# A one-column matmul that reads k early, behind the first four score matmuls of a chunked retention + mish feed-forward kernel

## Chip, cores and metric

One NeuronCore of one Trainium2 chip runs the whole program. The metric is the device time of one execution in microseconds (us); lower is better. Before the change the median of 3 runs was 192.03 us (191.44 to 192.17).

## What is computed

The inputs q, k and v have 4 batches, 8 heads, 768 positions and 64 dimensions. Per batch and head a decaying state is carried along the sequence, and its read-out goes through a feed-forward layer with the mish activation:

```python
gamma = 1.0 - 2.0 ** (-5.0 - np.arange(H))
for t in range(S):
    state = gamma * state + outer(k[:, :, t], v[:, :, t])
    y[:, :, t] = scale * (q[:, :, t] @ state)
x = y.transpose(0, 2, 1, 3).reshape(B * S, H * D)      # 3072 x 512
h = x @ w_in                                           # 512 -> 2048
g = h * tanh(log1p(exp(h)))
out = g @ w_out                                        # 2048 -> 512
```

## The kernel before, in words

**Tiles.** The recurrence is cut into 24 chunks of 128 positions (six per batch). Within a chunk the sum over earlier positions becomes a masked score matrix, and what came before the chunk arrives through the state. From the third block on, a chunk is cut once more into two halves of 64 positions, and TensorE (PE) is used as four 64x64 quarters: the score, state and read-out matmuls there are all 64x64, written so that four neighbours use the four quarters.

**Blocks.** The work is done in 11 blocks: block 0 has the four chunks 0 to 3, every later block n has the two chunks 2n+2 and 2n+3 (256 tokens). A block's first feed-forward product (`g1_seven`, matmuls at L818) and second one (`seven`, matmuls at L954) are written as seven smaller products each, with sums of operands made by VectorE (DVE). The order of work is written out by hand: `steps_of` and `steps_of_first` (L1314, L1355) list what is done at each named step ("at1", "m1", "m3" and so on) between the products of a block, and instructions run on each engine in the order of the program. So the attention of block n+1 is done inside block n: its scores at step "m1" (`scores_two`, L500 to L511), its mask at "m5", its read-out at "m7" (`y_of`, L521).

**Outer products.** `y_of(n)` reads the state (L542) and applies the masked scores (L553). Then `outers` (L485 to L498) makes the products of k and v that move the state on, for the chunks that `outers_at(n)` names: the two chunks of block n+1. In blocks 2 and earlier it names one chunk only, and the second one's outer products are made at step "m1" by `scores_and_outer` (L587), ahead of the scores there. The stationary operand of each outer product is k in half precision (tile `qk`), so its weight load (LDWEIGHTS) needs k of that chunk.

**How k arrives.** `bring_k` (L418 to L427) copies k of a chunk from HBM and turns it to half precision on the way: two DMAs of 64 KB on GpSimd's (POOL's) queue, the first for heads 0, 2, 4, 6 and the second for heads 1, 3, 5, 7. From block 2 on, step "m3" asks for both chunks of the block three further on, four DMAs in a row. Chunk 10 is asked for at "m3" of block 1, and chunk 11 at the end of step "at1" of block 2, behind the casts there. `cast_q` and `cast_v` (L414, L431) write q and v in half precision on POOL, and `turn_by_dma` (L443) transposes q and k of a chunk with a DMA on SyncE's (SP's) queue into the tile `qkt`, from which the score matmuls read.

**Waits.** Where PE's first outer product has to wait both for its own engine and for a k DMA, a separate EVENT_SEMAPHORE instruction stands in PE's queue ahead of the weight load and takes one of the two.

Of the kernel before, what the change touches and what calls it, by code (L numbers as in the profile page):

```python
# [16 lines left out]
def kernel(  # L17
# [9 lines left out]
    nc = tc.nc  # L27
# [6 lines left out]
    HP = H // 2  # L34
# [23 lines left out]
    def toks(c):  # L58
        return slice(c * HB, (c + 1) * HB)
# [75 lines left out]
    loaded, cast, qkts, ats, ams, states, us, ys, sus = {}, {}, {}, {}, {}, {}, {}, {}, {}  # L135
# [364 lines left out]
    def scores_two(blk):  # L500
        a = first[blk]
        at = ats[a] = atps.tile([P, 2, 2, HP, HB], FP32, name="at", tag="at")
        for n in range(2):
            qt, kt = qkts[a + n]
            for j in range(HP):
                for c in range(2):
                    for x in range(2):
                        o = slice(64 * x, 64 * x + 64)
                        nc.tensor.matmul(  # L509
                            at[toks(c), x, n, j], kt[o, j, toks(c)], qt[o, j, toks(c)],  # L510
                            start=True, stop=True, skip_group_check=True)  # L511

    def mask_two(blk):
# [69 lines left out]
    def outers_at(blk):  # L583
        a = first[blk]
        return [a + 2] if blk <= TURN else [g for g in (a + 2, a + 3) if g < NCK]

    def scores_and_outer(g):  # L587
        outers([g], atps, "at")
        scores_two((g - CPB) // 2 + 1)
# [724 lines left out]
    def steps_of(blk):  # L1314
# [3 lines left out]
        else:  # L1318
# [8 lines left out]
            "at5": [(store_due, 3), (sums_a, blk, A)],  # L1327
            "g7": [(sums_a, blk, B)],
            "m1": only((scores_two, nb)),
            "m5": [*only((mask_two, nb)), (sums_b, blk)],  # L1330
            "m6": [(sums_c, blk), *then((gate_s, blk)), (cast_q, a + 1)],
# [80 lines left out]
```

## Time and profile before

| what | value |
|---|---|
| median of 3 runs | 192.03 us (191.44 to 192.17) |
| the profiled execution: its own time | 191.71 us |
| the profiled execution: its span | 189.8 us |
| PE matmuls busy | 183.3 us, 97% of the span |
| DVE busy | 156.7 us, 83% |
| ACT busy | 126.0 us, 66% |
| POOL busy | 94.7 us, 50% |

The span runs from the first to the last recorded instruction; the execution's own time has 1.9 us more around it. In the profile "PE" is a matmul and "PEld" the weight load ahead of it, "<-" reads "written from", and a line number is that of the kernel before. "DMA to landing" is the time from a DMA's issue to the last of its semaphore increments.

### The profile page before, as it was taken

The page shows a single profiled execution, that of the slowest core. Times are in us where ns is not written, and L with a number is a line of the kernel's source. Part 1 is how long each engine was busy: PE and PEld are TensorE (multiplying, and loading weights), DVE is VectorE, ACT ScalarE, POOL GpSimd, SP SyncE. Part 2 cuts the span into 40 slices and gives each one's busy share as a digit, 9 for nine tenths or more (in the row PEclk, how much of TensorE's full clock was granted, in tenths as well). Part 3 has the DMA queues.
Part 4 walks back from the last instruction along what each step waited for, and adds up shares of the span by engine and source line. Part 5 has one row for each costly group of instructions (what it writes and reads, how often), then busy time and mean ns, then how long its engine had stood idle before and what let it go on. Part 6 is the DMA issues. An engine that isn't in the chain of part 4 may idle for free.

```text
span 189.8 us, 7746 instructions
## 1 busy us (share of the span) xinstructions
PE 183.3 (97%) x3298; PEld 156.9 (83%) x3298; DVE 156.7 (83%) x330; ACT 126.0 (66%) x244; POOL 94.7 (50%) x135
## 2 busy tenths in 40 slices
PE   6989999999999999999999999999999999999992
PEld 2667546875988988988988988988988988989981
DVE  3997899889899698797897897797897897796662
ACT  3362699463893983894883883983884974975960
POOL 6570205696767937934934935915925923000000
PEclk9999999999999999999999999999999999999999
DMA  4999999999999999999996996996997953300203
GB/s 165 351 369 406 405 406 279 269 217 147 186 195 281 193 264 217 175 192 170 176 184 148 159 176 196 207 233 40 196 205 106 155 152 60 114 3 12 102 0 111
DMA packets 95521, 36.17 MB, mean 191 GB/s; under 512 B 82560, under 2 KB 88960, under 8 KB 95488
## 3 DMA queue, kind: packets, MB, share of 16 engines
q1 hardware_dynamic: 74112, 32.78, 73.7%
q0 software_dynamic: 21088, 2.62, 21.7%
q8 instruction: 25, 0.41, 0.9%
q10 hardware_dynamic: 288, 0.30, 0.4%
q14 instruction: 8, 0.07, 0.1%
HBM read 27.30 MB, written 6.29 MB: 177 GB/s over the span
## 4 chain that ended last, share of the span: by engine, by line
PE 94%; DVE 3%; issue 1%; POOL 0%; ACT 0%; POOLq 0%; DVEq 0%
PE h_ps L818 34%; PE o_ps L954 32%; PE h_ps L687 6%; PE o_ps L1207 5%; PE at L457 2%; PE h_ps L1055 2%; PE o_ps L1267 2%; PE y_ps L542 2%; PE at L509 2%; PE u_ps L495 2%; DVE am L329 2%; PE y_ps L553 2%; PE t_ps L264 1%; DVE osb L975 1%; PE at L322 0%
## 5 line engine op out<-in xcount | busy, mean ns | idle before, releaser
L838 DVE TENSOR_TENSOR hsum<-h_ps,hsnap 128x512 f32<-128x512 f32 x60 | 38.6, 685 | 9.7 <-ACT hsnap L828 6.8
L828 ACT COPY hsnap<-h_ps 128x512 f32<-128x512 f32 x60 | 32.1, 589 | 10.0 <-PE h_ps L818 9.7
L818 PEld LDWEIGHTS <-wsum 128*128 128x128 f16 x640 | 36.2, 98 | 0.2
L833 ACT ACTIVATE g<-hsum 128x512 f16<-128x512 f32 x60 | 34.6, 642 | 0.6 <-DVE hsum L838 0.2
L954 PEld LDWEIGHTS <-gsum 128*128 128x128 f16 x320 | 30.4, 98 | 3.7
L818 PE MATMUL h_ps<-xsum,wsum 128*128 128x128 f16 x480 | 30.2, 219 | 0.0
L954 PE MATMUL o_ps<-tmat,gsum 128*128 128x256 f16 x240 | 29.5, 273 | 0.0
L818 PEld LDWEIGHTS <-win 128*128 128x128 f16 x480 | 28.2, 98 | 0.9
L426 POOL DMA_DIRECT2D qk<-in_k_dram x36 | 27.6, 781 | 0.0
L954 PEld LDWEIGHTS <-g 128*128 128x128 f16 x248 | 22.7, 98 | 2.5
L414 POOL TENSOR_TENSOR qk<-qf,qvs 128x512 f16<-128x512 f32 x20 | 21.5, 1077 | 0.2 <-issue 0.2
L431 POOL TENSOR_TENSOR v<-vf,qvs 128x512 f16<-128x512 f32 x20 | 21.2, 1085 | 0.0
L954 PE MATMUL o_ps<-wout,g 128*128 128x256 f16 (+1 forms) x168 | 20.8, 267 | 0.0
L818 PE MATMUL h_ps<-xt,win 128*128 128x128 f16 x320 | 19.6, 219 | 0.0
L603 POOL TENSOR_TENSOR stc<-suc,gcv 128x256 f16<-128x256 f32 x15 | 9.9, 663 | 15.7 <-DVE suc L598 15.7
L560 ACT COPY hsum<-y_ps 128x512 f32<-128x512 f32 x9 | 5.3, 585 | 18.4 <-PE y_ps L553 18.4
L975 DVE TENSOR_TENSOR osb<-o_ps,snap 128x256 f32<-128x256 f32 (+1 forms) x32 | 13.0, 413 | 5.0 <-PE o_ps L954 2.5
L439 POOL COPY gate<-gsum 128x1 f16<-128x1 f16 x10 | 1.8, 185 | 26.8 <-DVE gsum L925 26.8
L963 ACT COPY snap<-o_ps 128x256 f32<-128x256 f32 x31 | 11.4, 371 | 5.5 <-PE o_ps L954 5.3
L818 PE MATMUL h_ps<-xsum,win 128*128 128x128 f16 x160 | 12.3, 220 | 0.0
L818 PE MATMUL h_ps<-xt,wsum 128*128 128x128 f16 x160 | 12.2, 219 | 0.0
L833 ACT ACTIVATE g<-h_ps 128x512 f16<-128x512 f32 x20 | 12.0, 598 | 0.0
(142 smaller groups left out, 310.6 us busy)
## 6 DMA issues: line engine op xcount, KB each, us to landing
vf<-in_v_dram SPq DMA_DIRECT2D x24, 256.0 KB, 6.0
out_dram<-osb SPq DMA_DIRECT2D x22, 256.0 KB, 3.5
qf<-in_q_dram SPq DMA_DIRECT2D x20, 256.0 KB, 4.9
wi<-in_moe_w_in_dram SPq DMA_DIRECT2D x3, 1024.0 KB, 10.5
wt<-in_moe_w_out_dram SPq DMA_DIRECT2D x3, 1024.0 KB, 9.3
qk<-in_k_dram POOLq DMA_DIRECT2D x36, 64.0 KB, 4.7
qfirst<-in_q_dram SPq DMA_DIRECT2D x2, 512.0 KB, 4.3
kf<-in_k_dram SPq DMA_DIRECT2D x4, 256.0 KB, 5.0
```

Of the source, the lines that this page charges most:

```text
L414: nc.gpsimd.tensor_tensor(by_head(g, room16(g)[0]), by_head(0, loaded[g][0]), f.broadcast_to((P, 2, HP, D)), op=ALU.mult)
L426: nc.gpsimd.dma_start(room16(g)[1][:, x::2], src[:, HP * x:HP * x + HP])
L431: nc.gpsimd.tensor_tensor(room16(g)[2], loaded[g][2], vs.unsqueeze(2).broadcast_to((P, H, D)), op=ALU.mult)
L603: by.tensor_tensor(stcs[g], sus.pop(g), decay, op=ALU.mult)
L687: nc.tensor.matmul(h_ps[:, j], win(s, f, bp), xt(blk, bp), start=(bp == 0), stop=(bp == NBP - 1))
L818: nc.tensor.matmul(h_ps[g][:, f], w(g, f, d), x(d), start=first and f == 0 and d == 0, stop=d == n - 1, skip_group_check=True)
L828: nc.scalar.copy(x, h_ps)
L833: nc.scalar.activation(gt[:, fb:fb + FPS, j * P:(j + 1) * P], h, AF.Mish, scale=inv_boost3)
L838: nc.vector.tensor_tensor(h, h_ps, x, op=ALU.add)
L954: nc.tensor.matmul(t, x(f), w(f)[:, c], start=first and f == 0, stop=f == n - 1, skip_group_check=True)
L963: nc.scalar.copy(x[:, c], t)
L975: nc.vector.tensor_tensor(dst[:, c], t, plus[:, c], op=ALU.add)
```

## The change

Inside `scores_two(blk)`, after the four matmuls of chunk n = 0 and head pair j = 0, one matmul is put in for each chunk that `outers_at(blk)` names. Its stationary operand is the first head's k of that chunk, 64 positions by 64 dimensions; its moving operand is one column of the transposed q. It writes one column of the score tile, at a place (chunk n = 1, last head pair) that a later score matmul of the same call overwrites, so no result depends on its value.

```diff
@@ scores_two
                             at[toks(c), x, n, j], kt[o, j, toks(c)], qt[o, j, toks(c)],
                             start=True, stop=True, skip_group_check=True)
+                if n == j == 0:
+
+                    for g in outers_at(blk):
+                        nc.tensor.matmul(
+                            at[:64, 0, 1, HP - 1, :1], cast[g][1][:64, 0], qt[:64, 0, :1],
                             start=True, stop=True, skip_group_check=True)
```

In the compiled program the other engines' instructions are the same and in the same order. On PE 15 pairs of weight load and matmul are added: one in the scores of block 2, and two each in the scores of blocks 3 to 9. Each added weight load waits for the first k DMA of its chunk. In return the first outer product of a chunk in `y_of` no longer waits for that DMA: in 8 places the two waits become one, and the separate EVENT_SEMAPHORE goes. The waits for each chunk's second k DMA stay where they were, in `y_of`.

More of the change, by code (lines that the diff above doesn't have):

```diff
@@ L510, in scores_two @@
                             at[toks(c), x, n, j], kt[o, j, toks(c)], qt[o, j, toks(c)],
+                            start=True, stop=True, skip_group_check=True)
+                if n == j == 0:
+                    for g in outers_at(blk):
+                        nc.tensor.matmul(
+                            at[:64, 0, 1, HP - 1, :1], cast[g][1][:64, 0], qt[:64, 0, :1],
                             start=True, stop=True, skip_group_check=True)
```

## The prediction

> **What bounds the kernel now.** I read the page first, then the busy time by block, then the two rows that meet in this change: when PE reaches the scores, and when k lands.
>
> ```profile
> span 189.8 us, 7746 instructions
> PE 183.3 (97%) x3298; PEld 156.9 (83%) x3298; DVE 156.7 (83%) x330; ACT 126.0 (66%) x244; POOL 94.7 (50%) x135
> ...
> PEclk9999999999999999999999999999999999999999
> ...
> PE 94%; DVE 3%; issue 1%; POOL 0%; ACT 0%; POOLq 0%; DVEq 0%
> ```
>
> PE is busy for 97% of the span, and 94% of the chain that ended last is PE work. The next view is the busy time in stretches from one call of `scores_two` to the next (after the length: busy time of PE, PEld, DVE, ACT, POOL; then granted clock, DMA share, GB/s).
>
> ```profile
> 68.40:82.70 14.30, 14.28 (x305) 13.05 (x306) 12.29 (x27) 10.05 (x20) 9.98 (x14) 1.00 1.23 199
> 82.70:96.70 14.00, 14.00 (x297) 12.87 (x296) 11.95 (x26) 10.00 (x21) 8.51 (x12) 1.00 1.29 181
> 124.70:138.80 14.10, 14.10 (x297) 12.91 (x296) 11.93 (x26) 9.95 (x21) 8.52 (x12) 1.00 1.09 156
> ```
>
> PE is busy for the whole of a block (14.00 of 14.00 us). So there is no idle time on PE in which a new stop could hide, and a microsecond by which PE stands still in the middle is a microsecond at the end. DVE has some 2 us spare per block, ACT 4, POOL over 4: no other engine becomes late when PE stops.
>
> **What the added wait asks for.** In PE's queue everything behind a waiting weight load stands: the other 28 score pairs, the last group of L818, all of L954 of that block; and behind those ACT's copies, DVE's mask (L516), POOL's gates on DVE's sums, and with them SP's transposes. So the question is whether k is there. These are the eight groups of weight loads of the calls that get an added matmul (start, length), under a row with the time of a single load in ns (shortest, median, longest):
>
> ```profile
> L509 PEld LDWEIGHTS <-qkt x288: 102/110/110, 54.4 to 167.0; 64*64 64x64 f16 x144
> ...
> 54.36 0.37 PEld L509 LDWEIGHTS <-qkt 64*64 64x64 f16 x32
> ...
> 68.44 0.55 PEld L509 LDWEIGHTS <-qkt 64*64 64x64 f16 x32
> ...
> 82.69 0.33 PEld L509 LDWEIGHTS <-qkt 64*64 64x64 f16 x32 [0.21 <-issue]
> ...
> 96.70 0.34 PEld L509 LDWEIGHTS <-qkt 64*64 64x64 f16 x32 [0.21 <-issue]
> ...
> 110.71 0.33 PEld L509 LDWEIGHTS <-qkt 64*64 64x64 f16 x32 [0.21 <-issue]
> ...
> 124.68 0.33 PEld L509 LDWEIGHTS <-qkt 64*64 64x64 f16 x32 [0.21 <-issue]
> ...
> 138.81 0.33 PEld L509 LDWEIGHTS <-qkt 64*64 64x64 f16 x32 [0.21 <-issue]
> ...
> 152.82 0.33 PEld L509 LDWEIGHTS <-qkt 64*64 64x64 f16 x32 [0.21 <-issue]
> ```
>
> 32 loads take 0.33 us, the last one's own 0.11 among them, so a pair takes (0.33 - 0.11) / 31 = 0.007 us, and the place behind the first four is 0.03 us after each start. Below are the k DMAs that the last added load of each place waits for (the first DMA of chunks 8, 11, 13, 15, 17, 19, 21, 23), each with its issue time on POOL and, in the line under it, its time to landing.
>
> ```profile
> 50.11 0.81 POOL L426 DMA_DIRECT2D qk<-in_k_dram  x1
> DMA to landing us min/median/max: 4.2/4.2/4.2
> ...
> 66.27 0.81 POOL L426 DMA_DIRECT2D qk<-in_k_dram  x1
> DMA to landing us min/median/max: 4.9/4.9/4.9
> ...
> 77.44 0.76 POOL L426 DMA_DIRECT2D qk<-in_k_dram  x1
> DMA to landing us min/median/max: 5.8/5.8/5.8
> ...
> 91.46 0.77 POOL L426 DMA_DIRECT2D qk<-in_k_dram  x1
> DMA to landing us min/median/max: 4.6/4.6/4.6
> ...
> 105.51 0.77 POOL L426 DMA_DIRECT2D qk<-in_k_dram  x1
> DMA to landing us min/median/max: 5.3/5.3/5.3
> ...
> 119.49 0.77 POOL L426 DMA_DIRECT2D qk<-in_k_dram  x1
> DMA to landing us min/median/max: 5.6/5.6/5.6
> ...
> 133.45 0.77 POOL L426 DMA_DIRECT2D qk<-in_k_dram  x1
> DMA to landing us min/median/max: 4.9/4.9/4.9
> ...
> 147.62 0.77 POOL L426 DMA_DIRECT2D qk<-in_k_dram  x1
> DMA to landing us min/median/max: 2.9/2.9/2.9
> ```
>
> Place by place, landing against the place:
> - Block 2: 50.11 + 4.2 = 54.3, wanted at 54.39. No wait, with 0.1 us to spare.
> - Block 3: 66.27 + 4.9 = 71.2, wanted at 68.47. **PE stops for 2.7 us.** This is the chunk that block 2 asks for itself, only 2.2 us ahead of the place.
> - Block 4: 77.44 + 5.8 = 83.2, wanted at 82.72. A stop of 0.5 us.
> - Block 5: 96.1, wanted at 96.73. None.
> - Block 6: 110.8, wanted at 110.74. A stop of 0.1 us.
> - Block 7: 125.1, wanted at 124.71. A stop of 0.4 us.
> - Block 8: 138.35, wanted at 138.84. None.
> - Block 9: 150.5, wanted at 152.85. None.
>
> The sum of the stops is 2.7 + 0.5 + 0.1 + 0.4 = 3.7 us. The POOL work that leads to the issue of chunk 11 (q and v casts of step "at1") lies ahead of the stop and waits for nothing behind it, so its landing is not moved. From block 4 on the k DMAs are issued behind POOL's decay of the state, which waits for DVE and, through it, for the outer products on PE; so issue and place move together when PE is late, and what decides is the latency alone: the places of blocks 4 to 8 lie 5.2 to 5.4 us after the issue (82.72 - 77.44 = 5.28, 138.84 - 133.45 = 5.39), and the five latencies are 5.8, 4.6, 5.3, 5.6 and 4.9 us. They straddle the bound.
>
> **What the stop swallows.** In the place of block 3 the group of 32 loads takes 0.55 us where the others take 0.33: PE waits there for the second chunk's transpose, 0.2 us. Behind a stop of 2.7 us that wait is over, so 0.2 us come off. Nothing else is given back: from the scores at 68.44 to those at 82.69 it takes 14.25 us, from there to 96.70 it takes 14.01, and of the 0.24 us between them this wait is 0.22.
>
> **The added pairs.** 15 weight loads and 15 matmuls of one column. The trace shows no matmul of one column. Below, each could cost as little as the pair's pace, 15 x 0.007 = 0.1 us; above, a load that nothing overlaps costs its own 0.11 us, 15 x 0.11 = 1.65 us. Two neighbours of the added pair use the same quarter of the array, and four pairs are what goes by before a quarter's turn comes again, so I take 4 x 0.007 = 0.03 us each: 0.4 us. Where PE stands anyway part of it is hidden; I leave it in.
>
> **What is saved.** Eight of these eleven go:
>
> ```profile
> L495 PEldq EVENT_SEMAPHORE  x11: 51/51/51, 45.4 to 157.8; - x11
> ...
> 87.36 0.42 PEld L553 LDWEIGHTS <-v 64*64 64x64 f16 x32
> 87.74 0.39 PEld L495 LDWEIGHTS <-qk 64*64 64x64 f16 x32
> ```
>
> The last load of L553 starts at 87.36 + 0.42 - 0.10 = 87.68 and the first of L495 at 87.74: 0.06 us where the pace inside the group is (0.42 - 0.10) / 31 = 0.01 us. So the 51 ns are seen in full, and 8 x 0.05 = 0.4 us are saved; between 0 (the wait that stays, for PE's own semaphore, holds as long) and 0.5. It cancels the added pairs.
>
> **Sum.** 3.7 - 0.2 + 0.4 - 0.4 = +3.5 us. Against the profiled execution's own time this gives 191.71 + 3.5 = 195.2 us; that execution lies 0.32 us below the median of the runs, so for a median I say 192.03 + 3.5 = **195.5 us**. A measurement of this kernel tells about 0.5%, or 0.96 us, from no change.
>
> **Rivals.**
>
> 1. *Only the first stop costs.* While PE stands for 2.7 us the DMA queues empty, and the later k DMAs land earlier than they do now by 0.6 us or more. For it: the later stops are small (0.5, 0.1, 0.4), and three of the places have time to spare already. Against it: SP's loads and POOL's k DMAs of those blocks are issued behind PE's progress, so they meet in the same way as now. Without the 1.0 us of the later places: 192.03 + 2.5 = 194.5 us.
>
> 2. *The stop also lowers PE's clock.* The rows of the end of the span show the clock after PE's last matmul:
>
> ```profile
> 186.00:187.00 1.00, 0.16 (x3) 0.00 (x0) 0.49 (x3) 0.00 (x0) 0.00 (x0) 1.00 0.38 131
> ...
> 188.50:189.00 0.50, 0.00 (x0) 0.00 (x0) 0.00 (x0) 0.00 (x0) 0.00 (x0) 0.92 0.00 0
> 189.00:189.40 0.40, 0.00 (x0) 0.00 (x0) 0.00 (x0) 0.00 (x0) 0.00 (x0) 0.50 0.00 0
> ```
>
> PE works for the first 0.16 us from 186.00 and no more; the mean of 0.92 from 188.50 to 189.00 is a fall to 0.50 at 188.92, so 2.8 us after the last work. The stop of 2.7 us is just short of that. If the clock falls and comes back only after a stretch as long as it took to fall, some 2.8 us run at half speed and 1.4 us of work are lost: 195.5 + 1.4 = 196.9 us. The Trainium skill ("TensorE: Matmul & The Clock Gate", section "What's actually happening") says that the clock halves after an idle window of about 3.4 us, and that this window runs free of the kernel. By it a stop of 2.7 us alone does not halve the clock; the fall after 2.8 us here says that a window need not be wholly idle. By its figure the loss would be an estimated 1.7 us. I hold a fall for unlikely, since the stop is a little shorter than those 2.8 us.
>
> 3. *PE does not stop, and the change is not slower.* If k of chunk 11 landed by 68.47, the only long stop would be gone, and with it most of the cost. Two ways: the DMA is quicker in that run, or a waiting load lets other pairs pass it, so that the change does not do what it says. The point from which it decides is a latency of 2.2 us for that DMA. The fastest of all in this trace took 2.6:
>
> ```profile
> DMA to landing us min/median/max: 2.6/4.7/7.0
> ```
>
> With it PE would still stop for 66.27 + 2.6 - 68.47 = 0.4 us. Then the stops of the later places would have to be gone as well; the price is -0.4 us saved, +0.4 us for the pairs, +0 to +0.4 for the stop: 192.0 to 192.4 us, and 191.6 if the pairs cost nothing.
>
> 4. *Longer stops.* If all of the five latencies of blocks 4 to 8 were the longest of them, 5.8 us, each place would stop for some 0.5 us, 2.5 us in place of 1.0: 197.0 us.
>
> **How the numbers follow.** The forecast has 0.65, the first rival 0.15, the clock 0.11, the third rival 0.04, longer stops 0.05. The range reaches from 193.7 (first rival with 0.8 us less, should the DMA of chunk 11 take 4.1 us) to 197.3 (clock or longer stops, with the pairs at twice the price). Slower by over 0.5% is all but the third rival, 0.95; within 0.5% 0.04; faster 0.01.
>
> **What will show it.** In the profile after, L515 is the added matmul. Right: in the calls of `scores_two` of blocks 3, 4 and 7 PE's loads show idle time that a DMA of `qk` ended, some 2.7, 0.5 and 0.4 us, next to none in blocks 2, 5, 8 and 9; the stretch that begins with the place of block 3 is some 2.5 us longer, PEclk stays at 9; three EVENT_SEMAPHORE are left at L495. Wrong: if PE shows no idle time at the place of block 3, if the blocks from 96.70 on grow by over 0.6 us each, if PEclk shows less than 9 behind the stop, or if the pairs of L515 in places without a wait cost over 0.1 us each.

## The result and the profile after

The changed kernel takes 198.49 us, the median of 6 executions (196.81 to 200.47), against 192.29 us before (191.44 to 193.79, 6 executions): a ratio of 1.030, 95% interval 1.025 to 1.035. That is +6.2 us where +3.5 was forecast, and 1.2 us above the upper end of the range. The six fall in two groups by PE's granted clock: 196.81, 197.06 and 197.59 us with a clock of 1.00 throughout, and 199.38, 199.43 and 200.47 us with a mean of 0.983 to 0.991. The three at full clock alone lie 4.5 to 5.3 us above the median before. The profiled execution is the longest of the six; the ratios leave out executions over 1.5% above the fastest of their kernel (this one, and both with a lowered clock in the repeat below), so medians stand beside them.

The page of the kernel after, the lines that answer to those shown of before:

```profile
span 198.6 us, 7768 instructions
PE 187.2 (94%) x3313; PEld 159.1 (80%) x3313; DVE 157.1 (79%) x330; ACT 126.5 (64%) x244; POOL 95.4 (48%) x135
...
PEclk9999999999999975999999999999999999999999
...
PE 45%; DMA 23%; POOL 10%; ACT 6%; DVE 5%; SPq 5%; issue 4%; POOLq 0%; DVEq 0%
```

The span is 8.8 us longer. PE's share of the chain that ended last has gone from 94% to 45%: in five blocks the chain now runs from PE through a k DMA (the k DMAs are 14 of the 23% DMA) to the POOL work that issued it. And the clock row has a dent, 7 and 5, which before had not.

The weight loads of the added matmul (L515) in order of time; in brackets the idle time on PEld ahead of a load and what ended it:

```profile
73.12 0.12 PEld L515 LDWEIGHTS <-qk 64*64 64x64 f16 x1 [3.07 <-DMA qk<-in_k_dram]
...
90.61 0.10 PEld L515 LDWEIGHTS <-qk 64*64 64x64 f16 x1 [0.47 <-DMA qk<-in_k_dram]
...
119.11 0.10 PEld L515 LDWEIGHTS <-qk 64*64 64x64 f16 x1 [0.32 <-DMA qk<-in_k_dram]
...
133.46 0.10 PEld L515 LDWEIGHTS <-qk 64*64 64x64 f16 x1 [0.26 <-DMA qk<-in_k_dram]
```

These are blocks 3, 4, 6 and 7, the four that the forecast named: 3.1, 0.5, 0.3 and 0.3 us, 4.1 in sum against 3.7. (The expectation of `again` below has 4.5 us for the same stops: it counts each from the start of the load before it, 0.1 us earlier.) The other places show no wait at L515. The DMA of chunk 11 was issued at 67.7 and landed 5.3 us later, at 73.0 (the line of its source for the window of this issue; duration in ns, then first and last start):

```profile
L426 POOL DMA_DIRECT2D qk<-in_k_dram x1: 803/803/803, 67.7 to 67.7; - x1
...
DMA to landing us min/median/max: 5.3/5.3/5.3
```

Now the clock, by stretches around the stop that ends at 73.12 (the last three columns are clock, DMA share, GB/s):

```profile
72.00:72.50 0.50, 0.00 (x0) 0.00 (x0) 0.50 (x2) 0.00 (x0) 0.18 (x1) 0.88 1.07 221
...
74.00:74.50 0.50, 0.50 (x7) 0.50 (x6) 0.50 (x1) 0.00 (x0) 0.36 (x1) 0.50 0.60 116
...
79.00:79.50 0.50, 0.50 (x5) 0.42 (x4) 0.00 (x0) 0.00 (x0) 0.00 (x0) 0.79 0.00 0
```

A mean of 0.88 over half a microsecond is a fall to 0.50 at 72.38, while PE stood; 0.79 is a rise to 1.00 at 79.21. The clock was halved for 6.8 us, and PE worked for 6.1 of them, which is a loss of 3.0 us. Of the 8.8 us the stops are 4.1, the clock 3.0; 1.3 us more is a wait for a transpose in block 2, ahead of every added wait that held (the waits of the same profile: sum, times, longest):

```profile
PEld L509 <- DMA qkt<-qk: 1.3, 1, 1.3
```

Its k DMA was issued at 44.9, before the first added matmul, and took 5.9 us:

```profile
L426 POOL DMA_DIRECT2D qk<-in_k_dram x1: 747/747/747, 44.9 to 44.9; - x1
...
DMA to landing us min/median/max: 5.9/5.9/5.9
```

The repeat (0.6 us) and `x0_first_not3` (0.8) show the same wait; `landed`, `not_block3`, `chunk11_early` and `both_early`, which have a matmul at that place too, show none. `block3_late`, which has no added matmul in block 2, shows it as long as here (1.3 us). So the wait does not need the change; the one profile of the kernel before does not have it, and how often it comes there stays open. `x0_first_not3` has it and is no slower for it. The rest is 0.4 us. The added pairs account for about that much: the stretch from scores to scores in which nothing waits is 14.06 us long (104.60 to 118.66) against 14.01 (96.70 to 110.71 before).

### The profile page after: what moved, and what is told of

It is laid out like the page before. It is cut to its first block, busy times and chain, and to the rows that moved or that the text cites. A ratio compares the mean times of both kernels' runs of the same rounds, so it can differ in the third digit from the quotient of the medians.

```text
span 198.6 us, 7768 instructions
## 1 busy us (share of the span) xinstructions
PE 187.2 (94%) x3313; PEld 159.1 (80%) x3313; DVE 157.1 (79%) x330; ACT 126.5 (64%) x244; POOL 95.4 (48%) x135
## 4 chain that ended last, share of the span: by engine, by line
PE 45%; DMA 23%; POOL 10%; ACT 6%; DVE 5%; SPq 5%; issue 4%; POOLq 0%; DVEq 0%
PE o_ps L960 24%; PE h_ps L824 15%; DMA qk<-in_k_dram 14%; DMA wi<-in_moe_w_in_dram 6%; POOL qk L426 3%; SPq L278 3%; POOL qk L414 3%; POOL v L431 3%; DMA qkt<-qk 3%; ACT g L709 2%; PE y_ps L548 2%; SPq L190 1%; PE at L509 1%; PE y_ps L559 1%; POOL stc L609 1%
## 5 line engine op out<-in xcount | busy, mean ns | idle before, releaser
L960 PEld LDWEIGHTS <-gsum 128*128 128x128 f16 x320 | 31.5, 100 | 4.3
L960 PE MATMUL o_ps<-tmat,gsum 128*128 128x256 f16 x240 | 31.2, 283 | 0.0
L960 PE MATMUL o_ps<-wout,g 128*128 128x256 f16 (+1 forms) x168 | 21.4, 273 | 0.0
```

The costliest lines, as they stand in the source:

```text
L960: nc.tensor.matmul(t, x(f), w(f)[:, c], start=first and f == 0, stop=f == n - 1, skip_group_check=True)
```

## The experiments

**The change once more** (`again`, no edit), for another execution's profile.

> The changed kernel, unaltered, for a profile at full clock. Theory A (k lands behind the place that now waits for it; stops of 3.1, 0.6, 0.4 and 0.3 us in the profile after, 4.5 us in sum) says +4.3 to +4.8 us in an execution whose clock is 1.00 throughout, with the longest stop at the scores of block 3. Theory B (the stop lets the clock fall) says that executions split in two: some at 1.00, some 1.7 us later for each 3.4 us spent at half clock (+6 to +8 us). Rival C (the added pairs cost over 0.1 us each) would show groups of L509 that are 0.2 us longer in places where PE does not wait.

198.27 us median of 4 against 192.38: two executions at a clock of 1.00 (194.94 and 197.69 us) and two lower (0.991 and 0.990: 198.86 and 199.50 us). The profile is that of the one at 197.69, and its stops are:

```profile
72.16 0.10 PEld L515 LDWEIGHTS <-qk 64*64 64x64 f16 x1 [2.30 <-DMA qk<-in_k_dram]
...
86.74 0.10 PEld L515 LDWEIGHTS <-qk 64*64 64x64 f16 x1 [0.43 <-DMA qk<-in_k_dram]
...
116.21 0.10 PEld L515 LDWEIGHTS <-qk 64*64 64x64 f16 x1 [1.29 <-DMA qk<-in_k_dram]
...
130.66 0.10 PEld L515 LDWEIGHTS <-qk 64*64 64x64 f16 x1 [0.30 <-DMA qk<-in_k_dram]
```

4.3 us in sum, the same four places, other sizes: the stop of block 6 is 1.3 us where it was 0.3. Its DMA (first half of chunk 17) took 6.6 us to land, where the same one took 5.6 in the profile above:

```profile
L426 POOL DMA_DIRECT2D qk<-in_k_dram x1: 760/760/760, 109.6 to 109.6; - x1
...
DMA to landing us min/median/max: 6.6/6.6/6.6
```

A stop of 2.3 us left the clock at 1.00 here. The four places of theory A and the split of theory B hold, but neither execution at full clock lies where A's numbers put it: they are +2.6 and +5.3 us, not +4.3 to +4.8. In the profiled one 0.6 us is the wait for a transpose in block 2.

**Block 3 alone, and all but block 3.**

```diff
-                    for g in outers_at(blk):
+                    for g in (outers_at(blk) if blk == TURN + 1 else []):    # block3_only
+                    for g in (outers_at(blk) if blk != TURN + 1 else []):    # not_block3
```

> The added matmuls are kept in the scores of block 3 alone (2 of 15). Theory A: the stop of about 3 us stays, the other three go: +2.9 to +3.2 us at full clock. Theory B: the clock falls in some executions still, which then stand at +4.7 to +6.2 us. Rival C (pairs): 2/15 of the cost only, under +0.5 us.

195.37 us median of 6 against 192.38 (+3.0); ratio 1.016 (1.011 to 1.021). Clock 1.00 in two executions (194.71 and 195.05), 0.988 to 0.991 in four (195.25 to 197.53). Theory A and B hold in kind, both with smaller numbers than expected: +2.3 and +2.7 us at full clock, +2.9 to +5.2 below it. The profiled execution stopped for 1.9 us only, since its k DMA took 4.2 us to land (5.3 in the profile after), and even so its clock fell.

```profile
70.72 0.10 PEld L515 LDWEIGHTS <-qk 64*64 64x64 f16 x1 [1.90 <-DMA qk<-in_k_dram]
```

```profile
71.00:71.50 0.50, 0.50 (x27) 0.46 (x12) 0.50 (x2) 0.00 (x0) 0.41 (x1) 0.76 1.27 290
...
74.50:75.00 0.50, 0.50 (x6) 0.40 (x5) 0.00 (x0) 0.00 (x0) 0.00 (x0) 0.83 0.08 9
```

It fell at 71.26, half a microsecond after PE was at work again, and rose at 74.67: 3.41 us at half rate, 1.7 us lost.

> The added matmuls are kept everywhere but in the scores of block 3 (13 of 15). Theory A: only the short stops are left, +0.8 to +1.5 us. Theory B: no stop is longer than 1 us, so the clock is 1.00 in every execution and the times do not split. Rival C (pairs): 13/15 of the cost, over +3.5 us.

195.56 us median of 6 (193.97 to 197.01; +3.2); ratio 1.013 (1.008 to 1.018). The clock is 0.996 or more in all six, as theory B has it. But the time is twice what theory A had expected from the profile after. Its stops:

```profile
112.77 0.10 PEld L515 LDWEIGHTS <-qk 64*64 64x64 f16 x1 [1.11 <-DMA qk<-in_k_dram]
...
128.31 0.10 PEld L515 LDWEIGHTS <-qk 64*64 64x64 f16 x1 [1.38 <-DMA qk<-in_k_dram]
```

Blocks 6 and 7 again, with DMAs of 6.4 and 6.6 us. Rival C (pairs) would give this time too; the next run parts them. By the medians the two halves add up to the whole, +3.0 and +3.2 to +6.2; with a spread of some 3 us in each, that they do so to a tenth is luck.

**The pairs without a wait.**

```diff
-                    for g in outers_at(blk):
+                    for g in range(a, a + len(outers_at(blk))):
```

> The same 15 matmuls in the same places, but each reads k of a chunk of the block itself, which PE has used before, so that none waits; the 8 EVENT_SEMAPHORE stay. Theory A: only the pairs' own work, 15 x 0.03 = +0.4 us, no measurable change, clock 1.00. Rival C (pairs): as slow as the change, over +3.5 us.

192.71 us median of 12 against 192.38; ratio 1.001 (0.998 to 1.004). No idle time ahead of L515. Rival C falls: the pairs are worth 0.3 us of the 6 by the medians, and 0.8 us at most by the interval.

**Chunk 11 asked for earlier**, the whole change otherwise.

```diff
-                "at1": [(gate_x, blk), (cast_v, a - 1), (cast_q, a), (cast_v, a), (bring_k, a + 1)],
+                "at1": [(gate_x, blk), (bring_k, a + 1), (cast_v, a - 1), (cast_q, a), (cast_v, a)],
```

> The change with all its 15 added matmuls, and in block 2 the DMAs of chunk 11 issued ahead of POOL's three casts of step at1 instead of behind them, 3 us earlier. Theory A (what counts is when k lands against the place): chunk 11 lands about 0.5 us ahead of the place of block 3 to 0.5 us behind it, the stop there is gone, and what is left is that of the version without block 3: +2.5 to +3.2 us. Theory B: with no stop of 2 us or more the clock stays at 1.00 in every execution. Rival D (the added wait costs at block 3 for another reason, for example that PE must switch to other weights there): as slow as the change, +5 to +6 us.

195.16 us median of 4 (194.80 to 195.56) against 192.22; ratio 1.015 (1.013 to 1.017): as expected, and 3.3 us less than the change. The clock is 0.997 to 1.00. The DMA of chunk 11 was issued 4.8 us ahead of its place (64.0 against 68.83) where it had 2.2 us, but took 5.6 us, so a stop of 0.7 us is left at block 3:

```profile
69.67 0.10 PEld L515 LDWEIGHTS <-qk 64*64 64x64 f16 x1 [0.73 <-DMA qk<-in_k_dram]
```

Three shorter stops stand elsewhere: 0.2 us in block 2, 0.5 in block 4 and 1.1 in block 6, 2.5 us in all four. Rival D falls.

**The first halves first**, without block 3. `bring_two` issues the four DMAs of step "m3" in another order.

```diff
+    def bring_two(g):
+        for x in range(2):
+            for n in (g, g + 1):
...
+                    nc.gpsimd.dma_start(room16(n)[1][:, x::2], src[:, HP * x:HP * x + HP])
...
-                "m3": [*only((y_end,)), (bring_k, a + 2), (bring_k, a + 3)],
+                "m3": [*only((y_end,)), (bring_two, a + 2)],
```

> The version without the matmuls of block 3, and in step m3 the four k DMAs in another order: the first halves of both chunks ahead of the second halves, so that the DMA that the second added load waits for is issued 0.73 us earlier. Theory A: the place then lies 6.0 us behind the issue in place of 5.25, and of latencies of 4.3 to 6.7 us (five profiles) few reach that: the short stops shrink from 1.0 to 2.9 us in sum to 0.1 to 0.8, time +0.2 to +1.0 us. If the latency of a DMA comes from what was issued ahead of it on POOL's queue, the gain is all 0.73 us per place; if it lands no earlier since the queue is shared, the time stays at +2.5 to +3.2.

192.62 us median of 12; ratio 1.000 (0.998 to 1.002): 13 of the 15 matmuls at the places of the change, and no cost left. 0.73 us more of lead per place takes away the 3.2 us of the version without it. No place waits: the DMA that the second added load needs took up to 5.7 us in this profile, which 5.25 us would not have covered and 6.0 us do.

**A longer stop**, with block 3's matmuls alone.

```diff
-                "at1": [(gate_x, blk), (cast_v, a - 1), (cast_q, a), (cast_v, a), (bring_k, a + 1)],
+                "at1": [(gate_x, blk), (cast_v, a - 1), (cast_q, a), (cast_v, a), (cast_v, a),
+                        (cast_v, a), (bring_k, a + 1)],
```

> The version with the added matmuls of block 3 alone, and chunk 11 asked for 2.1 us later (two of POOL's v casts are done twice more ahead of it, with the same values). Theory A: the stop grows by 2.1 us, from 2.0-3.1 to 4.1-5.2. Theory B: a stop of over 4 us lets the clock fall in every execution (clock 0.98 to 0.99, none at 1.00), against 4 of 6 with the shorter stop, and the time is +5.8 to +8.5 us. If the clock does not depend on the length of the stop, some executions keep 1.00.

199.48 us median of 4 (197.91 to 200.77; +7.3); ratio 1.035 (1.031 to 1.039). No execution keeps a clock of 1.00: 0.991 once, 0.983 three times. The stop is 5.3 us, a little more than expected, and the clock, after falling at 74.0, rises at 80.84, 6.8 us later (0.58 over one microsecond). 1.3 us of the time of the profiled execution is the wait for a transpose in block 2. The stop and the clock:

```profile
75.27 0.12 PEld L515 LDWEIGHTS <-qk 64*64 64x64 f16 x1 [5.30 <-DMA qk<-in_k_dram]
```

```profile
73.00:74.00 1.00, 0.00 (x0) 0.00 (x0) 0.00 (x0) 0.00 (x0) 1.00 (x3) 1.00 1.71 154
74.00:75.00 1.00, 0.00 (x0) 0.00 (x0) 0.00 (x0) 0.00 (x0) 0.47 (x1) 0.50 1.93 116
...
80.00:81.00 1.00, 1.00 (x8) 0.72 (x6) 0.00 (x0) 0.37 (x1) 0.00 (x0) 0.58 0.00 0
```

**A later place** for the same 15 matmuls, in the kernel before.

```diff
+        for g in outers_at(blk):
+            nc.tensor.matmul(
+                other[:64, 1, 0, 0, 0, :1], cast[g][1][:64, 0], qkts[a][0][:64, 0, :1],
+                start=True, stop=True, skip_group_check=True)
         present_of(False, other)
```

> The kernel before with the 15 one-column matmuls at another place: in the read-out of the block, behind the 32 state matmuls of L542 and ahead of the masked scores, 4.5 us later than in the change. k has landed by then in every profile, and the 8 EVENT_SEMAPHORE ahead of the outer products go as in the change. Theory A: no stop; -0.4 us for the EVENT_SEMAPHORE and +0.4 us for the pairs, so no measurable difference (-0.5 to +0.5 us), clock 1.00.

192.13 us median of 12 against 192.22; ratio 1.000 (0.997 to 1.003). No wait, three EVENT_SEMAPHORE left, and nothing gained or lost, as expected.

**Both reorderings**, the whole change otherwise.

> All 15 added matmuls at the places of the change, with both reorderings of the k DMAs: chunk 11 ahead of POOL's casts in block 2, and in step m3 the first halves of both chunks ahead of the second ones. Theory A: nothing of the change but its waits costs time, and they are nearly all met: a stop of 0 to 0.9 us is left at block 3 (latency of 5.6 us in the run with chunk 11 asked for early), none or little elsewhere: +0.2 to +1.2 us, clock 1.00. If the cost lay in the place itself, +2 us and more.

193.30 us median of 12 against 193.03; ratio 1.0055 (1.002 to 1.009). All 15 matmuls stand where the change put them; one stop is left, 0.2 us longer than expected because its DMA took 6.0 us, and the clock is 0.996 or more in all executions. What is left of the cost is +0.3 us by the medians and 0.4 to 1.7 us by the ratio, about that stop.

```profile
69.73 0.10 PEld L523 LDWEIGHTS <-qk 64*64 64x64 f16 x1 [1.11 <-DMA qk<-in_k_dram]
```

## Why the prediction was wrong

**The mechanism was right.** PE stops where it was said to, for the reason given: asking for k earlier takes the cost away with the matmuls left in place, a part of it in `chunk11_early`, nearly all in `x0_first_not3` and `both_early`, and reading k that is there (`landed`) costs nothing measurable. The first stop was forecast at 2.7 us and was 3.1, 2.3 and 1.9 in three profiles, with latencies of 5.3, 4.6 and 4.2 us where the forecast had 4.9.

**The step that failed is "How the numbers follow": the clock.** It stood as a rival with a chance of 0.11 and a price of 1.4 us, held for unlikely since the stop "is a little shorter than those 2.8 us" after which the clock fell at the end of the span. Those 2.8 us were one sample and no bound: from PE's last work to the fall it was 2.2 us in the change and 3.9 in `block3_late`. By the mean clock it fell in 3 of 6 executions of the change, in 2 of 4 of the repeat and in 4 of 6 of `block3_only`, once after a stop of 1.9 us, while a stop of 2.3 us let it stand. So the length of the stop does not decide alone. That the stop is the cause is shown by `not_block3` and `chunk11_early`, where no execution is below 0.996, and by `block3_late`, where all are. The counts are a little uncertain, since the mean also holds the fall at the end of the span: of the 23 executions of the kernel before that stand beside `block3_late`, two have 0.992, close to the 0.991 that counts as a fall here.

The price is 1.7 us or about 3, not 1.4: the halved stretches measured 3.41 us (`block3_only`) and 6.8 us (the change and `block3_late`), one and two times the same length. In the two long ones PE was still idle for part of the first 3.4 us; that this is what makes the second follow is consistent with three profiles and was not tested by itself. The Trainium skill ("TensorE: Matmul & The Clock Gate", section "What's actually happening") has the window of 3.4 us and that it runs free of the kernel; the 3.41 us agree, and the 6.8 us as two windows. The Trainium skill's advice on the same page, in the section "Why this matters for your kernels", to keep gaps below some 3 us is not enough here: the clock fell after 1.9 us, and the measurement decides.

The clock is not all of the miss. Of the 2.7 us by which the median cost exceeds the forecast, 1.3 are there in the executions at full clock too (median 197.06 us, +4.8); the other 1.4 come from the three with a lowered clock.

**The term that was mis-sized: the later stops.** The "1.0 us of the later places" came from five latencies of one execution (4.6 to 5.8 us) against a bound of 5.25. That they straddle the bound was seen, and that this makes the sum a matter of chance was not carried into the forecast, only into a rival with 0.05. Over the profiles the same DMAs took up to 6.6 us, and the short stops added up to 1.1 us (the change), 1.8 (`chunk11_early`), 2.0 (the repeat) and 2.5 (`not_block3`, where the median cost was +3.2 us). A wait never gives time back when the DMA is early, so by this argument the spread adds to the mean. In the two profiles of the whole change all stops together were 4.1 and 4.3 us against the 3.7 of the sum, so this term alone does not make the miss at full clock; the wait in block 2 (1.3 and 0.6 us) stands beside it, and the forecast had no term for that. The first rival, by which these stops vanish, was wrong.

**The term that was wrong without weight: the saving.** The EVENT_SEMAPHORE were to be worth 0.4 us. In the change eight of the eleven went:

```profile
L495 PEldq EVENT_SEMAPHORE  x3: 51/51/51, 45.5 to 68.6; - x3
```

In block 4 the gap ahead of the outer products shrank, from 0.06 to 95.62 - (95.27 + 0.42 - 0.10) = 0.03 us, but the group behind it grew from 0.39 to 0.41 us:

```profile
95.27 0.42 PEld L559 LDWEIGHTS <-v 64*64 64x64 f16 x32
95.62 0.41 PEld L495 LDWEIGHTS <-qk 64*64 64x64 f16 x32
96.07 0.33 PEld L960 LDWEIGHTS <-g 128*128 128x128 f16 x4
```

From the first load of the masked scores to the next product it is 96.07 - 95.27 = 0.80 us. Before it was 88.17 - 87.36 = 0.81:

```profile
88.17 0.11 PEld L954 LDWEIGHTS <-g 128*128 128x128 f16 x2
```

So a saving of 0.01 us was left of 0.05 in this block. Over the five blocks from the scores of block 4 to those of block 9, `landed` (pairs, no saving) takes 0.38 us longer than the kernel before and `x0_first_not3` (pairs and saving, no wait) 0.24, one profile each: 0.03 us a block. Both say that the 51 ns were not lost in full; that they lay beside work of the array is an inference. `late_place` does not test it, since pairs and saving were to cancel there; its blocks are 0.01 us longer than before.

**What held.** 0.4 us for the pairs: in a block without a wait the stretch is 0.05 us longer for two pairs. That PE gives nothing back: behind the stop of `block3_only` the blocks are as long as before, within 0.01 us. And that the long stop swallows the wait for the second chunk's transpose: behind the stop of 2.3 us the 28 loads left follow in 0.32 us.

## What to carry to other kernels

A read that is put early on an engine that is busy throughout is a wait put early: compare its place with the landing of the data, execution by execution, and where latencies straddle the bound add the mean of what lies above it, not the sum of one profile. A stop of about 2 us on PE can cost as much again by the clock, so price it before calling it unlikely. And a wait instruction that looks like 50 ns of lost time may already lie beside other work; the time from group to group says so, the gap alone does not.

## What the runs showed of the hardware that was not expected

- The granted clock fell in an execution (`block3_only`) whose added wait stopped PE for 1.9 us (at 71.26, when PE had been back at work for half a microsecond), and stood in one (`again`) with a stop of 2.3 us.
- It stayed down for 3.41 us or for 6.8 us. No execution of `not_block3` or `chunk11_early`, whose profiles show stops of at most 1.4 us at the added matmuls, was below 0.996.
- The time to landing of one and the same k DMA (first half of chunk 17) was 5.3 us in the kernel before, 5.6 with the change, 6.6 in its repeat and 6.4 in `not_block3`, at the same place of the program.
